# A fourth buffer for pairs of weight words, one pair loaded earlier in the first tile, and retention steps handed out more often in the second tile

## The chip, the core and the metric

The kernel runs on one core of a Trainium2 chip. The metric is device time in microseconds (us). A core has five engines that run at the same time and wait for each other through semaphores: TensorE (matmuls, PE in the profile, its weight loads PEld), VectorE (DVE), ScalarE (ACT), GpSimd (POOL) and SyncE (SP), which here only issues transfers. Each engine works through its own list of instructions strictly in the order in which the program wrote them; this program fixes that order by hand (a manual schedule). An instruction that has to wait holds up everything behind it on its engine.

## What is computed

The inputs are q, k and v of 8 batches, 8 heads, 576 positions and 64 dimensions, and four weight matrices. The first part is a retention layer (attention without a softmax, with a decay by distance), the second a feed-forward layer with a maximum over three projections:

```python
scores = (1 / np.sqrt(D)) * np.matmul(q, k.transpose(0, 1, 3, 2))
gamma = 1.0 - 2.0 ** (-5.0 - np.arange(H))
Dmat = np.where(rel >= 0, gamma[:, None, None] ** rel[None], 0.0)    # rel = position of q - position of k
attn = np.matmul(scores * Dmat[None], v)
x = attn.transpose(0, 2, 1, 3).reshape(B * S, H * D)                 # 4608 x 512
h = np.maximum(np.maximum(x @ w1, x @ w2), x @ w3)                   # w1..w3: 512 x 768
out = h @ w_out                                                      # w_out: 768 x 512
```

The weights arrive as 64-bit floats. The kernel reads them as pairs of 32-bit words ("bits") and converts them to 32-bit floats itself.

## The kernel before

**Tiles.** The 4608 rows of x are cut into nine tiles of 512 rows (`NT`), each made of four chunks of 128 rows (`CPT = 4`). While the feed-forward layer of tile t runs, the retention of tile t + 1 is computed between its matmuls. `steps(t + 1)` gives twelve slots with the retention's parts (`load`, `transposes`, `decay`, `scores`, `values`, ...), and the generator `ffn(t)` yields between them. The loop at the end of the program takes one slot, then lets `ffn` go on to its next yield. So the first tile's feed-forward (t = 0) runs with `steps(1)`, which has its own branch with chunks a, b, c, d = 4, 5, 6, 7 (lines 924 to 939). From chunk 7 on (`BY_PE`), q and k are transposed on VectorE out of blocks that `load_blocks` has fetched in small pieces (lines 214 and 221), one buffer pair each for q and k. Earlier chunks are transposed on TensorE.

**First tile: weights.** `pieces` lists the weights in blocks of 128 columns: 18 for the three projections, then 6 for w_out. Two blocks form a pair, 1 MB, which lies in one tile `bits` of the pool `wraw`; its buffers are `WAHEAD // 2`, which is 3. `load_weights(n)` (line 485) issues the next n blocks on SP, a projection block in two transfers (line 499), a block of w_out in one (line 494). Three pairs are loaded ahead of the first tile. After that, `product`, the last step of converting a pair, calls `load_weights`, so that each converted block starts the load of one block three pairs later. `convert_all` is the conversion as a generator: `exponent` (lines 630, 632), `fraction` (638, 639, 641), `whole` (644), `sign` (648) and `product` (656) for each pair, on VectorE and ScalarE; `ffn(0)` advances it between its matmul groups (`up_plain`, line 784) and then multiplies h by w_out (`downs_plain`, line 771). When all pairs are converted, the pools of the conversion are closed, and a pool called `late` takes over their memory, for sums of weights, of x and of h.

**Second tile and after: fewer products.** From tile 1 on, two of the three pairs of hidden blocks (in tile 1) or all three (later) are computed by `up`. It replaces a part of the block products by sums of blocks of x and of the weights: a list of 20 `PRODUCTS` in five accumulating chains named A to E (line 760). After a step of a chain, ScalarE copies the chain's bank to a tile `part` or into h (line 745), and VectorE joins such parts (line 748). Each product is two matmul pairs, and the generator `up` yields after each of them, so a hidden pair has 40 steps.

**Who hands out the retention's VectorE work.** From tile 1 on, `soon` does not issue a step of the retention at once but appends it to the queue `urgent` (`spread` is set). This holds for VectorE's transposes (line 194 by the profile, since they are issued from `chore`), the masks, the sums of states, the scaled values xT, the sums of x, and also for `load`, whose transfers then are issued by SP. `chore()` takes one step from `urgent`, or, when that is empty, from `chores` (sums of weights). In `ffn(t)` with t > 0, the loop over the steps of `up` decides when:

```python
elif step % 4 == 1 or step % 4 == 3 and len(urgent) > 6:
    chore(len(urgent) > 0)
elif step % 4 == 2 and chores and (t > 1 or NF // 2 - 1 not in summed_fp):
    chores.popleft()()
```

So one retention step is handed out at every fourth step, and a second one, two steps later, while more than six wait. Anything left over is handed out all at once ahead of the next `scores` or `values`. The order in which this happens is the order of VectorE's and SP's lists.

Of the kernel before, what the change touches and what calls it, by code (L numbers as in the profile page):

```python
# [77 lines left out]
WAHEAD = 6  # L78
# [3 lines left out]
def kernel(  # L82
# [32 lines left out]
    ppool = ctx.enter_context(tc.tile_pool(name="ppool", bufs=PARTS))  # L115
    opool = ctx.enter_context(tc.tile_pool(name="opool", bufs=2))
    while_converting = ExitStack()
    wraw = while_converting.enter_context(tc.tile_pool(name="wraw", bufs=WAHEAD // 2))
    wtmp = while_converting.enter_context(tc.tile_pool(name="wtmp", bufs=2))
    raw0 = while_converting.enter_context(tc.tile_pool(name="raw0", bufs=1))  # L120
    ps_r = ctx.enter_context(tc.tile_pool(name="ps_r", bufs=4, space=PSUM))
# [63 lines left out]
    late, chores, urgent, scaling, spread = {}, deque(), deque(), deque(), []  # L185

    def scale(n=1):
        for _ in range(min(n, len(scaling))):
            scaling.popleft()()  # L189

    def chore(n=1):
        for _ in range(n):
            if urgent or chores:
                (urgent or chores).popleft()()
# [59 lines left out]
    def transposes(g):  # L254
        both = qks[g] = {}
        if g >= BY_CHUNKS:
            for n, tag in (("k", "kT"), ("q", "m1")):
                both[n] = att.tile([P, H, D], FP32, tag=tag, name=n + "T", bufs=2 if n == "k" else 3)
        else:
            both["k"] = att.tile([P, NP, C], FP32, tag="kT", name="kT", bufs=2)  # L260
            both["q"] = ppool.tile([P, NP, C], FP32, tag="part", name="qT")
        if g >= BY_PE:
            for n in ("k", "q"):
                soon(partial(nc.vector.transpose, both[n][:].rearrange("a p c -> a (p c)"),
                             raws.pop(("kx" if n == "k" else n, g))[:].rearrange("a x y i -> a (x y i)")))
            return
        for n, src in (("k", raws["k", g]), ("q", raws.pop(("q", g)))):
            pool, tag = (ps_r, "r") if g >= CPT else (ps_x, "x")
            pt = pool.tile([P, NP, C], FP32, tag=tag, name=n + "t")
            for p in range(NP):  # L270
                nc.tensor.transpose(pt[:, p, :], pair(src, p), ident[:C, :C])
            nc.scalar.copy(both[n][:], pt[:])
# [449 lines left out]
    def late_room():  # L722
        pool = late["pool"]
        late["W"] = [pool.tile([P, NF, P], FP32, name=f"n{n}") for n in range(1, 9)]
        late["X"] = {n: pool.tile([P, NH], FP32, name=n)[:] for n in sorted({x[0] for x in X_SUMS})}
# [3 lines left out]
    def convert(n):  # L729
        for _ in range(n):  # L730
            next(converting, None)
# [47 lines left out]
    def up_plain(t, h, fb, i):  # L779
        ps = (ps_x, ps_y)[fb % 2].tile([P, NT], FP32, tag="xy"[fb % 2], name="up")  # L780
        first_of_all = t == 0 and (fb, i) == (0, 0)
        for cols in (slice(0, NT - C), slice(NT - C, NT)) if first_of_all else (slice(0, NT),):
            for dc in range(NDC):
                nc.tensor.matmul(ps[:, cols], lhsT=w_sb[i, fb][:, dc * P:(dc + 1) * P], rhs=xT[t][:, dc, cols],  # L784
                                 start=dc == 0 and cols.start == 0, stop=dc == NDC - 1,
                                 skip_group_check=first_of_all)
        if i > 0:
            return lambda: nc.vector.tensor_tensor(h[:, fb, :], h[:, fb, :], ps[:], op=ALU.max)
        return lambda: nc.scalar.copy(h[:, fb, :], ps[:])

    def ffn(t):

        h = hpool.tile([P, NF, NT], FP32, tag="h", name="h")
        if t == 0:
            for fp, i in units:
                for fb in (2 * fp, 2 * fp + 1):
                    maximum = up_plain(t, h, fb, i)
                    if CPT not in qks:
                        maximum()
                        transposes(CPT)  # L800
                        convert(4)
                        continue
                    if (fp, i) == units[-1]:
                        maximum()
                        convert(2)
                        continue
                    convert(4 if (fp, i) in units[:2] else 2)
                    maximum()
                yield
            convert(3)  # L810
            for fb, _ in enumerate(downs_plain(t, h)):
                convert(2 if fb < 2 else 4 * len(pieces))
                if fb == 2:
                    while_converting.close()
                    late["pool"] = ctx.enter_context(tc.tile_pool(name="late", bufs=1))
                    late_room()
                    sums_of_outs()
                elif fb > 2:
                    chore({3: 4, 4: 0, 5: 2}[fb])
                if fb in (1, 3):  # L820
                    yield
            yield
            return
        if t == 1:
            spread.append(True)
            weight_sums(0)
            weight_sums(2)
        plain = 1 if t == 1 else None
        order = (1, 0, 2) if t == 1 else (0, 2, 1)
        total = sum(48 if fp == plain else 2 * len(PRODUCTS) for fp in order)  # L830
        count = parts = 0
        for fp in order:
            if fp != plain:
                while fp not in summed_fp:
                    chore()
            for step, cost in enumerate(up_plain_all(t, h, fp) if fp == plain else up(t, h, fp)):
                if fp == plain:
                    chore(4 if step == 4 else 8)
                elif step % 4 == 1 or step % 4 == 3 and len(urgent) > 6:
                    chore(len(urgent) > 0)  # L840
                elif step % 4 == 2 and chores and (t > 1 or NF // 2 - 1 not in summed_fp):
                    chores.popleft()()
                if step % 3 == 2:
                    scale()
                count += cost or 1
                if count * (NF // 2 * 3) >= (parts + 1) * total:
                    parts += 1
                    yield
            sums_of_hidden(h, fp)
            if fp == plain:  # L850
                weight_sums(fp)
        chore(len(urgent))
        for n, _ in enumerate(downs(t, h, order)):
            chore(4)
            scale(2)
            if n in (1, 3):
                yield
        yield
# [52 lines left out]
    def steps(t):  # L911


        todo = [[] for _ in range(3 * CPT)]

        def at(n, *what):
            for step, *args in what:
                if step is values:
                    if args[0][0] < NG:
                        todo[n].append(partial(values, *args))  # L920
                elif args[0] < NG:
                    todo[n].append(partial(soon, partial(step, *args)) if step is load else partial(step, *args))

        if t == 1:
            a, b, c, d = range(CPT, 2 * CPT)
            at(0, (load, b))
            at(1, (scores, a), (state, a), (keep, a))
            at(2, (transposes, b), (decay, b), (load, c))
            at(3, (scores, b), (load_blocks, d, 0))
            at(4, (decay, c), (load_blocks, d, 1, 2))  # L930
            at(5, (values, [a, b], [b, c]), (load_blocks, d, 3), (load, d))
            at(6, (keep, c), (transposes, c), (load_blocks, d + 1, 0))
            at(7, (transposes, d), (decay, d), (load_blocks, d + 1, 1, 2))
            at(8, (scores, c), (scores, d), (load_blocks, d + 1, 3), (load, d + 1))
            at(9, (load_blocks, d + 2, 0, 1))
            at(10, (decay, d + 1), (load_blocks, d + 2, 2))
            at(11, (values, [c, d], [d]), (load_blocks, d + 2, 3), (load, d + 2),
               (transposes, d + 1))
            return todo
        for n in range(0, CPT, 2):  # L940
            a, b, m = CPT * t + n, CPT * t + n + 1, 6 * (n // 2)
            first_pair = a == BY_CHUNKS
            s = m + 2 if first_pair else m + 1
            at(m - (t == 2 and n > 0), (transposes, b))
            if first_pair:
                at(m, (decay, b), (load, a + 2), (carry, a))
            at(s, (scores, a), (scores, b), (load, b + 2))
            at(s + 1, (decay, a + 2))
            at(s + 2, (decay, b + 2))
            at(s + 3, (values, [a, b]), (transposes, a + 2), (load, a + 4))  # L950
        return todo
# [58 lines left out]
```

## Time and profile before

| what | value |
|---|---|
| median of 4 runs | 756.0 us (755.84 to 757.13) |
| the profiled execution's own time | 757.13 us |
| its span, first to last instruction | 755.1 us |
| granted TensorE clock | 1.000 |
| TensorE busy | 744.3 us (99% of the span) |
| VectorE busy | 509.1 us (67%) |
| ScalarE busy | 319.5 us (42%) |
| GpSimd busy | 82.2 us (11%) |
| first tile's feed-forward, first up matmul to last down matmul | about 27 to 126 us |
| second tile | about 126 to 209 us |
| transfers in the first 60 us | 217 to 225 GB/s, the 16 transfer engines 96 to 100% busy |

In a timeline line the columns are: start in us, duration in us, engine, line, operation, what is written and read, tile shapes, and how many instructions were merged; in square brackets, the idle time of the engine just before it and what ended that idle time. A line of the table of waits reads: who waited, for whom, us in total, how often, and the longest. "SPq" is the issuing of a transfer on SP.

### The profile page before, as it was taken

The numbers are of one execution on the slowest core, as the hardware profiler recorded it, in microseconds if no ns is written. First come the engines' busy times: TensorE is split into PE (matmuls) and PEld (weight loads), VectorE is DVE, ScalarE is ACT, GpSimd is POOL, SyncE is SP. The second block draws the span as 40 slices with busy tenths as digits, with TensorE's granted clock in tenths as the row PEclk, the third lists the DMA queues.
The fourth block names the chain that finished last, engine by engine and source line by source line (L and its number), as shares of the span: only waits on it lengthen the run. The fifth ranks groups of instructions, "written<-read, shape, count | busy, mean of one in ns | idle before, by whom it ended". The sixth has DMA issues, their size and how long they took to land.

```text
span 755.1 us, 16567 instructions
## 1 busy us (share of the span) xinstructions
PE 744.3 (99%) x6728; PEld 607.5 (80%) x6728; DVE 509.1 (67%) x856; ACT 319.5 (42%) x645; POOL 82.2 (11%) x103
## 2 busy tenths in 40 slices
PE   7999999999999999999999999999999999999998
PEld 6645545588888888888888888888888888888887
DVE  2898897858876866677567647675667656763662
ACT  3575531064245443544355435542454245414441
POOL 3110113001000110011010101010101010100000
PEclk9999999999999999999999999999999999999999
DMA  9995762504242414242243324142415141000001
GB/s 214 225 237 122 203 145 68 101 2 79 64 99 43 82 46 100 56 72 56 69 88 63 64 60 95 32 83 63 88 35 98 43 93 36 1 30 29 0 1 56
DMA packets 230204, 59.30 MB, mean 79 GB/s; under 512 B 210800, under 2 KB 228848, under 8 KB 230128
## 3 DMA queue, kind: packets, MB, share of 16 engines
q1 hardware_dynamic: 229264, 57.91, 35.4%
q8 instruction: 53, 0.87, 0.5%
q10 hardware_dynamic: 864, 0.33, 0.2%
q14 instruction: 23, 0.19, 0.1%
HBM read 48.76 MB, written 9.44 MB: 77 GB/s over the span
## 4 chain that ended last, share of the span: by engine, by line
PE 95%; DVE 2%; DMA 2%; SPq 1%; issue 0%; ACT 0%; ACTq 0%; DVEq 0%
PE a L760 18%; PE b L760 15%; PE dx L557 11%; PE up L784 11%; PE c L760 8%; PE dz L557 5%; PE d L760 5%; PE e L760 5%; PE sk L307 3%; PE down L771 3%; PE dy L557 3%; PE o L424 2%; PE o L431 2%; DMA qraw<-in_q_dram 1%; PE kv L310 1%; PE s L285 1%
## 5 line engine op out<-in xcount | busy, mean ns | idle before, releaser
L748 DVE TENSOR_TENSOR part<-part 128x512 f32<-128x512 f32 x161 | 111.2, 691 | 108.4 <-ACT part L745 106.0
L745 ACT COPY part<-b 128x512 f32<-128x512 f32 x115 | 67.3, 586 | 154.7 <-PE b L760 154.7
L748 DVE TENSOR_TENSOR h<-h,part 128x512 f32<-128x512 f32 x115 | 80.3, 698 | 29.3 <-ACT h L745 25.4
L784 PE MATMUL up<-xT,w 128*128 128x512 f32 (+2 forms) x200 | 84.8, 579 | 1.5 <-DVE w L656 1.5
L745 ACT COPY part<-a 128x512 f32<-128x512 f32 x92 | 53.9, 585 | 49.6 <-PE a L760 49.1
L784 PEld LDWEIGHTS up<-xT,w 128*128 128x128 f32 x200 | 36.7, 190 | 43.7 <-issue 39.9
L760 PE MATMUL a<-s,w 128*128 128x256 f32 x276 | 70.9, 380 | 0.0
L760 PE MATMUL b<-s,n 128*128 128x256 f32 x276 | 70.8, 379 | 0.0
L189 ACT ACTIVATE vraw<-vraw,gk 128x64 f32<-128x64 f32 x208 | 65.6, 346 | 3.5 <-DMA vraw<-in_v_dram 3.4
L760 PEld LDWEIGHTS b<-s,n 128*128 128x128 f32 x276 | 52.5, 190 | 7.1
L760 PEld LDWEIGHTS a<-s,w 128*128 128x128 f32 x276 | 52.4, 190 | 7.1
L527 POOL TENSOR_TENSOR H<-h 128x256 f32<-128x256 f32 x24 | 20.2, 842 | 308.7 <-DVE h L748 308.7
L760 PE MATMUL c<-xT,w 128*128 128x256 f32 x184 | 49.1, 389 | 0.0
L760 PE MATMUL b<-xT,n 128*128 128x256 f32 x184 | 47.2, 379 | 0.0
L760 PE MATMUL d<-s,w 128*128 128x256 f32 x184 | 47.2, 379 | 0.0
L324 POOL TENSOR_TENSOR s<-s,gs_of 64x512 f32<-64x512 f32 x21 | 22.2, 1055 | 213.7 <-DVE s L322 209.2
L557 PE MATMUL dx<-To,H 128*128 128x256 f32 (+1 forms) x204 | 44.9, 371 | 0.0
L760 PE MATMUL e<-xT,w 128*128 128x256 f32 x184 | 43.5, 379 | 0.0
L760 PE MATMUL a<-xT,n 128*128 128x256 f32 x184 | 43.5, 379 | 0.0
L557 PEld LDWEIGHTS dx<-To,H 128*128 128x128 f32 x204 | 36.6, 190 | 4.8
L760 PEld LDWEIGHTS e<-xT,w 128*128 128x128 f32 x184 | 35.0, 190 | 5.2 <-DVE s L322 0.2
L760 PEld LDWEIGHTS b<-xT,n 128*128 128x128 f32 x184 | 35.0, 190 | 4.7
(122 smaller groups left out, 1283.8 us busy)
## 6 DMA issues: line engine op xcount, KB each, us to landing
bits<-in_moe_w_dram SPq DMA_DIRECT2D x36, 256.0 KB, 5.4
out_dram<-osb SPq DMA_DIRECT2D x35, 256.0 KB, 2.1
kraw<-in_k_dram SPq DMA_DIRECT2D x32, 256.0 KB, 3.2
vraw<-in_v_dram SPq DMA_DIRECT2D x32, 256.0 KB, 3.6
qraw<-in_q_dram SPq DMA_DIRECT2D x224, 32.0 KB, 2.2
kxraw<-in_k_dram SPq DMA_DIRECT2D x224, 32.0 KB, 2.1
bits<-in_moe_w_out_dram SPq DMA_DIRECT2D x6, 512.0 KB, 5.9
qraw<-in_q_dram SPq DMA_DIRECT2D x6, 256.0 KB, 5.3
```

The lines of the kernel that those rows point to most:

```text
L189: scaling.popleft()()
L307: nc.tensor.matmul(s[half(c), h, :], lhsT=kT[half(c), h, :], rhs=qT[half(c), h, :], start=True, stop=True)
L324: nc.gpsimd.tensor_tensor(new, new, factor, op=ALU.mult)
L424: nc.tensor.matmul(o[m][half(c), n, u, :], lhsT=vds[g][half(m), h, :], rhs=sts[g][half(m), h, :], start=n == 0 and u == 0, stop=place(g, m ...
L431: nc.tensor.matmul(o[m][half(c), n, u, :], lhsT=stacks[g][half(m), h, :], rhs=qks[g]["q"][half(m), h, :], start=False, stop=True, skip_gro ...
L527: urgent.append(lambda: (pool(s3, a11, a21, op=ALU.subtract), pool(s4, a12, s2, op=ALU.subtract)))
L557: nc.tensor.matmul(o, lhsT=hS[n](fp)[:, m * P:(m + 1) * P], rhs=late["T"][n][:, fp, cols], start=first and fp == order[0] and (m == 0 or l ...
L745: nc.scalar.copy(of[step], ps[step[0]][:])
L748: nc.vector.tensor_tensor(of[dst], a, b, op=op)
L760: nc.tensor.matmul(ps[chain][:, e, :], lhsT=factor(w, 2 * fp + e), rhs=xS[t][x], start=n == 1 and e == 0, stop=ends, skip_group_check=True)
L771: nc.tensor.matmul(b[:], lhsT=h[:, fb, m * P:(m + 1) * P], rhs=w_sb["out", fb], start=(fb == 0), stop=(fb == NF - 1))
L784: nc.tensor.matmul(ps[:, cols], lhsT=w_sb[i, fb][:, dc * P:(dc + 1) * P], rhs=xT[t][:, dc, cols], start=dc == 0 and cols.start == 0, stop= ...
```

## The change

Three edits:

- The pool `wraw` has four buffers for pairs of weight words instead of three (`WAHEAD // 2 + 1`).
- In the third slot of `steps(1)`, during the first tile's feed-forward, `load_weights(2)` loads one more pair right after chunk c's load. From there on, each load of a pair is for the pair four ahead of the one just converted, instead of three ahead.
- In the second tile (t = 1) alone, the second retention step of every four is handed out while more than two wait, not only while more than six wait. In the other tiles the bound stays six.

```diff
-    wraw = while_converting.enter_context(tc.tile_pool(name="wraw", bufs=WAHEAD // 2))
+    wraw = while_converting.enter_context(tc.tile_pool(name="wraw", bufs=WAHEAD // 2 + 1))
...
-                elif step % 4 == 1 or step % 4 == 3 and len(urgent) > 6:
+                elif step % 4 == 1 or step % 4 == 3 and len(urgent) > (2 if t == 1 else 6):
                     chore(len(urgent) > 0)
...
-            at(2, (transposes, b), (decay, b), (load, c))
+            at(2, (transposes, b), (decay, b), (load, c), (load_weights, 2))
```

No arithmetic changes, and no instruction is added or taken away on TensorE, VectorE, ScalarE or GpSimd.

## The prediction

> **What bounds the kernel now.** I read the page first (busy shares, then the chain that ended last), then TensorE's own waits in the second tile and after, then the timelines of TensorE, VectorE and the SP queue around each of those waits.
>
> From the page, engine shares and the chain by engine:
>
> ```profile
> PE 744.3 (99%) x6728; PEld 607.5 (80%) x6728; DVE 509.1 (67%) x856; ACT 319.5 (42%) x645; POOL 82.2 (11%) x103
> ...
> PE 95%; DVE 2%; DMA 2%; SPq 1%; issue 0%; ACT 0%; ACTq 0%; DVEq 0%
> ```
>
> TensorE is the bound: 95% of the last chain is its work. A busy PE row says little by itself, because matmul ends are modelled, but the chain runs from one matmul group straight into the next nearly everywhere. So a change that removes no matmul can only win the places where TensorE waits. TensorE's waits from 125 us to the end are a single line:
>
> ```profile
> PE sk L307 <- DVE qT L194: 1.0, 1, 1.0
> ```
>
> One wait in 630 us. In the timeline of TensorE it stands between the two chunks whose scores are computed in the middle of the second tile:
>
> ```profile
> 174.12 0.23 PE L310 MATMUL kv<-vraw,kraw 64*64 64x64 f32 x2
> 175.39 0.33 PE L307 MATMUL sk<-qT,kT 64*64 64x64 f32 x3 [1.04 <-DVE qT L194]
> ```
>
> The page counts 1.04 us idle, from the modelled end of one matmul. These small matmuls follow each other about every 0.06 us (the pair before starts at 174.11), so without the wait the second chunk would start at 174.17. The slot lost is 175.39 - 174.17 = 1.22 us. TensorE's weight loads wait 1.2 us for the same qT.
>
> VectorE's timeline ahead of it shows why qT is late:
>
> ```profile
> 163.29 1.28 DVE L194 TENSOR_TENSOR xT<-o,gq 128x512 f32<-128x512 f32 x2
> 166.14 2.14 DVE L748 TENSOR_TENSOR part<-part 128x512 f32<-128x512 f32 x3 [1.56 <-ACT part L745]
> 168.20 0.70 DVE L194 STREAM_TRANSPOSE kT<-kxraw 128x512 f32<-128x512 f32 x1
> 168.82 0.65 DVE L748 TENSOR_TENSOR h<-h,part 128x512 f32<-128x512 f32 x1
> 169.40 1.41 DVE L748 TENSOR_TENSOR part<-part 128x512 f32<-128x512 f32 x2
> 170.72 0.70 DVE L194 STREAM_TRANSPOSE qT<-qraw 128x512 f32<-128x512 f32 x1
> 171.35 2.17 DVE L748 TENSOR_TENSOR h<-h,part 128x512 f32<-128x512 f32 x3
> 173.44 0.68 DVE L748 TENSOR_TENSOR part<-e,part 128x512 f32<-128x512 f32 x1
> 174.04 0.70 DVE L194 STREAM_TRANSPOSE kT<-kxraw 128x512 f32<-128x512 f32 x1
> 174.66 0.67 DVE L194 STREAM_TRANSPOSE qT<-qraw 128x512 f32<-128x512 f32 x1
> ```
>
> VectorE works in order and is full from 166.14 to 175.26. Just before, it is idle 1.56 us for an ACT copy. The four transposes are the retention steps that line 839 hands out.
>
> **Second edit, the retention steps.** It adds no instruction. In the built order of the changed kernel the first chunk's kT and qT stand right behind the two xT, ahead of the three part sums; the second kT stands ahead of the three h joins, the second qT behind them. Working through with the starts above (start to start: transpose 0.62, one h 0.60, two parts 1.32, three h 2.09):
> - First pair: 164.5 to 165.8, wholly inside the 1.56 us of idle, so the part sums still start at 166.14. Their inputs were issued on SP by 146 us and land in 2 to 3 us, so the early place waits for no transfer.
> - Then three parts to 168.20, h to 168.80, two parts to 170.12, second kT to 170.74, three h to 172.83, second qT to 173.46.
> - 173.46 is 0.71 us before TensorE can use it (174.17). The wait goes: 1.22 us.
>
> A rule speaks against it. The third h join also releases a GpSimd difference (H L527, 0.73 us), which in the new order runs beside that second qT. The Trainium skill, "SBUF — State Buffer", section "Who interferes with whom", says VectorE and GpSimd share a port pair as an exclusive lock, the loser blocked for a whole instruction, for VectorE's two-port modes and its two-input operations. The trace shows such a case: an h join at 178.36 takes 1.51 us instead of 0.69 beside a GpSimd multiply at 178.28. Were qT held so, it would end at 173.46 + 0.73 = 174.19 and the gain be 1.2 less 0.02 plus a semaphore's 0.05, about 1.15. But transposes at 124.88 to 127.49 run beside GpSimd work and keep 0.70 and 0.67, so I take the row: 1.22. What may be held is the H sum behind it, 0.3 us, and that is covered.
>
> What becomes late: the e join moves from 173.44 to about 173.9. Its bank is wanted by chain d at 182.72 (181.5 after the gain), over 6 us of cover; with that cover gone it would cost its 0.5. SP's next loads wait for the first qT and are issued near 166 instead of 171.45; their data, and the values that ACT scales, come earlier, and ACT has idle time for them. From 187.00 VectorE's run starts from an ACT copy of TensorE's own output, so it shifts along with TensorE and no new wait appears.
>
> **First edit, the fourth buffer and the early load.** It adds 8 KB a partition and no transfer; every pair from the eighth on is issued one place earlier. What is late now is this (VectorE's timeline, then SP's; the DMA wait is for the first output weights):
>
> ```profile
> 88.02 0.69 DVE L630 TENSOR_SCALAR expo<-bits 128x1024 int32<-128x1024 int32 x1 [2.31 <-DMA bits<-in_moe_w_out_dram]
> ...
> 97.56 0.69 DVE L788 TENSOR_TENSOR h<-h,up 128x512 f32<-128x512 f32 x1 [0.93 <-PE up L784]
> 98.16 0.69 DVE L630 TENSOR_SCALAR expo<-bits 128x1024 int32<-128x1024 int32 x1
> 98.77 1.23 DVE L648 SCALAR_TENSOR_TENSOR expo<-bits,expo 128x1024 int32<-128x1024 int32 x1
> 100.03 1.23 DVE L656 TENSOR_TENSOR w_out<-mant,expo 128x1024 f32<-128x1024 f32 x1
> ```
> ```profile
> 60.08 2.97 SPq L499 DMA_DIRECT2D bits<-in_moe_w_dram  x4
> 63.10 4.36 SPq L214 DMA_DIRECT2D qraw<-in_q_dram  x8
> ```
>
> - Gained off the path: VectorE's waits for bits, 0.70 (at 79.46) and 2.31 us, and ACT's of 0.60, 2.37 and 1.41, should vanish. None is on TensorE's path. VectorE then only waits longer at the next point that TensorE sets: the max at 97.56.
> - The one TensorE wait near, 0.35 us at 101.31 for the first w_out, stays: it is max end of up (97.54) to product (101.26), 3.72 us in a row on VectorE, and the change moves none of these instructions. The bound from above, if it did go, is the start-to-start loss: 93.82 + 6.97 (a group of 16) = 100.79 against 101.31, 0.5 us.
> - The first loads into the fourth buffer (near 30 us) no longer wait for VectorE; SP's waits on line 499 are 3.0 us in all (2.1 and 0.9). The transfer engines are full until 60 us, so the order of arrival is as before: nothing.
> - Cost on SP: four more issues, 2.97 us, ahead of chunk 7's blocks (54.88 on). The blocks end two issues late: 79.6 + 1.2 = 80.8, and land at 83.0 by the median of 2.2. VectorE wants them at 84.42 (83.7 once the 0.70 is gone), TensorE the transposes at 91.84, 6.1 us after they end now (85.72). Covered. Their bytes are 1 MB; at the mean of 207 GB/s from 45 to 65 us that is 5.1 us of transfer. "DMA: Bandwidth & Descriptors", section "Measured", gives 6.15 us for 1 MB: an estimate by it adds one more microsecond, and both leave the path untouched.
>
> **Sum.** 1.22 + 0 = 1.2 us, between 0 (the gap refills elsewhere) and 1.7 (both gaps). The profiled execution took 757.13 us around a span of 755.1; its span becomes 753.9, its time 755.9. It is the slowest of four; against the median of 756.0 I forecast 754.8, or -0.16%. About 0.2% (1.5 us) is what a measurement of this kernel can tell from no change.
>
> **Rivals.**
> - The gap refills, or was particular to this execution (the other three are 1.0 to 1.3 us faster than it): gain 0 to 0.6, 755.4 to 756.0. For it: VectorE carries the same work, only in another order. Against: 0.71 us of margin, and no other TensorE wait for 500 us.
> - More than counted: the 0.5 at 101.31 goes too, or the second chunk's matmuls (1.19 us against 0.99 for the first) run as the first: 1.7, so 754.3. Against: the 3.72 us of VectorE do not move.
> - Slower: the early bits delay chunk 7's blocks. It decides once they land after 90.5 (then kT and qT end past 91.84), 7.5 us behind the 83.0 expected; to end 1.5 us above now it must also eat the 1.2, landing near 93.2: 757.6 or more. For it: the longest such block took 7.1 us to land. Against: even that lands at 87.9.
>
> **How the numbers follow.** Forecast case 0.70, by itself 754.4 to 755.2; refill 0.15; more 0.08; slower 0.07. The range of 754.2 to 756.3 leaves the slow case and little else out. Faster by over 0.2% needs below 754.5: the "more" case and the lower edge of the forecast, 0.21. Slower than 757.5: 0.07. The rest, 0.72, within.
>
> **What would show it.** Right: no wait of sk for qT near 174; transposes at 164.5 to 165.8, part sums still near 166.1; no VectorE wait for bits of the output weights; the 0.35 at the first down still there; SP's loads of the third tile from near 166. Wrong: a new TensorE wait before 126 us, part sums pushed past 166.5, or a wait for a bank after 176.

## The result, and the profile after

| | before | after |
|---|---|---|
| median, us | 756.3 (755.11 to 759.18) | 755.0 (753.70 to 757.81) |
| ratio of the times, with its 95% interval | | 0.9983 [0.9977, 0.9988] |
| span of the profiled execution, us | 755.1 | 752.7 |
| its own time, us | 757.13 | 754.70 |

The kernel became faster by 0.17%, 1.3 us. The forecast was 754.8 us, or 0.16% less.

The two profiled executions differ by more than that, 2.4 us of span, so the first step is to see where the difference lies. I cut TensorE's timeline at its landmarks. "First up" is the first product of the feed-forward layer, "first down" the first product with w_out, "sk" and "a" are where the second tile computes both chunks' scores and goes on to the next chain, and "last dx" is the start of the last run of products with w_out, whose bank is called dx:

| from, to | before | after | difference |
|---|---|---|---|
| start of the span to first up | 26.87 | 25.50 | -1.37 |
| first up to first down | 74.44 | 74.44 | 0.00 |
| first down to the second tile's first up | 24.29 | 24.30 | +0.01 |
| to the first sk | 47.58 | 47.58 | 0.00 |
| first sk to the next chain a (the scores of two chunks) | 3.40 | 2.02 | -1.38 |
| to the last dx | 572.92 | 572.90 | -0.02 |
| the tail behind it | 5.60 | 5.96 | +0.36 |

I don't count the start as the change's doing. Until the first up both kernels issue the same work. In the execution of before, TensorE waited 1.93 us for the third chunk's q to arrive; in that of after it didn't. This start lay at 25.6 to 26.9 us in the five profiles with three buffers and at 24.7 to 26.1 in the nine with four, so the profiles alone would leave room for an effect of the buffer. The times speak against it: the buffer alone gains nothing (below). I take as the profile's own answer the sum of the five middle rows, -1.39 us, 0.18% of 756, which is the measured ratio. All of it lies in one row.

The page of after, engine shares and the chain by engine, says as little about this as before's did:

```profile
PE 745.0 (99%) x6728; PEld 608.8 (81%) x6728; DVE 509.6 (68%) x856; ACT 319.1 (42%) x645; POOL 83.5 (11%) x103
...
PE 96%; DVE 1%; DMA 1%; issue 1%; SPq 0%; ACT 0%; ACTq 0%; DVEq 0%
```

TensorE's table of waits for the whole span of after (who waited, for whom, us in total, times, longest) does:

```profile
PE up L784 <- DVE w L656: 1.5, 1, 1.5
PE warm L153 <- POOL ident masks.py:199: 1.4, 1, 1.4
PE s L285 <- ACT qT L272: 0.6, 1, 0.6
PE o L393 <- POOL vd L249: 0.5, 1, 0.5
PE down L771 <- DVE w_out L656: 0.4, 1, 0.4
PE o L393 <- PE kv L352: 0.2, 1, 0.2
```

The row of sk waiting for qT is gone and no row of the second tile has taken its place: the two waits of o, which before's table does not have, lie ahead of the first up. The row of the first down is still there. VectorE's timeline around the second tile's transposes:

```profile
161.93 1.28 DVE L194 TENSOR_TENSOR xT<-o,gq 128x512 f32<-128x512 f32 x2
163.13 0.70 DVE L194 STREAM_TRANSPOSE kT<-kxraw 128x512 f32<-128x512 f32 x1
163.75 0.67 DVE L194 STREAM_TRANSPOSE qT<-qraw 128x512 f32<-128x512 f32 x1
164.77 2.14 DVE L748 TENSOR_TENSOR part<-part 128x512 f32<-128x512 f32 x3 [0.35 <-ACT part L745]
166.95 0.69 DVE L748 TENSOR_TENSOR h<-h,part 128x512 f32<-128x512 f32 x1
167.56 1.41 DVE L748 TENSOR_TENSOR part<-part 128x512 f32<-128x512 f32 x2
168.89 0.70 DVE L194 STREAM_TRANSPOSE kT<-kxraw 128x512 f32<-128x512 f32 x1
169.52 2.17 DVE L748 TENSOR_TENSOR h<-h,part 128x512 f32<-128x512 f32 x3
171.61 0.70 DVE L194 STREAM_TRANSPOSE qT<-qraw 128x512 f32<-128x512 f32 x1
172.24 0.55 DVE L525 TENSOR_TENSOR H<-h 128x256 f32<-128x256 f32 x1
172.71 0.68 DVE L748 TENSOR_TENSOR part<-e,part 128x512 f32<-128x512 f32 x1
```

Take 1.37 us off every predicted time, for the earlier start. Then the first pair was due at 163.1 to 164.4 and ran from 163.13 to 164.42. The part sums were due at 164.77 and started there: the transposes used up idle time, of which 0.35 us is left of 1.56. The second qT was due to end at 172.09 and ended at 172.31.

TensorE's timeline, at the first down and at the second chunk's scores:

```profile
99.94 14.00 PE L771 MATMUL down<-w_out,h 128*128 128x512 f32 x32 [0.37 <-DVE w_out L656]
...
172.74 0.23 PE L307 MATMUL sk<-qT,kT 64*64 64x64 f32 x2
172.80 0.22 PE L307 MATMUL sk<-qT,kT 64*64 64x64 f32 x2
```

The sk follow each other at 0.06 us. TensorE reaches them at 172.74, so qT has 0.43 us to spare.

In the first tile, VectorE's timeline of after:

```profile
83.88 0.66 DVE L630 TENSOR_SCALAR expo<-bits 128x1024 int32<-128x1024 int32 x1
...
96.17 0.69 DVE L788 TENSOR_TENSOR h<-h,up 128x512 f32<-128x512 f32 x1 [2.05 <-PE up L784]
96.78 0.69 DVE L630 TENSOR_SCALAR expo<-bits 128x1024 int32<-128x1024 int32 x1
97.38 1.25 DVE L648 SCALAR_TENSOR_TENSOR expo<-bits,expo 128x1024 int32<-128x1024 int32 x1
98.66 1.23 DVE L656 TENSOR_TENSOR w_out<-mant,expo 128x1024 f32<-128x1024 f32 x1
```

The exponent at 83.88 is the one that waited 2.31 us for bits before. It waits for nothing now, and the time comes back as idle time at the next point that TensorE sets: 2.05 us ahead of the max, where it was 0.93. The row from max to product is as long as it was, and the first down still waits 0.37 us for it.

### The profile page after: what moved, and what is told of

It is laid out like the page before. It is cut to its first block, busy times and chain, and to the rows that moved or that the text cites. A ratio compares the mean times of both kernels' runs of the same rounds, so it can differ in the third digit from the quotient of the medians.

```text
span 752.7 us, 16566 instructions
## 1 busy us (share of the span) xinstructions
PE 745.0 (99%) x6728; PEld 608.8 (81%) x6728; DVE 509.6 (68%) x856; ACT 319.1 (42%) x645; POOL 83.5 (11%) x103
## 4 chain that ended last, share of the span: by engine, by line
PE 96%; DVE 1%; DMA 1%; issue 1%; SPq 0%; ACT 0%; ACTq 0%; DVEq 0%
PE a L760 19%; PE b L760 16%; PE up L784 11%; PE dx L557 11%; PE c L760 8%; PE e L760 5%; PE d L760 5%; PE dz L557 5%; PE sk L307 3%; PE down L771 3%; PE dy L557 3%; PE o L424 2%; PE o L431 2%; PE s L285 1%; PE kv L310 1%; PE o L393 1%
## 5 line engine op out<-in xcount | busy, mean ns | idle before, releaser
L760 PEld LDWEIGHTS a<-xT,n 128*128 128x128 f32 x184 | 35.0, 190 | 4.7
```

What stands on the lines that cost most here:

```text
L760: nc.tensor.matmul(ps[chain][:, e, :], lhsT=factor(w, 2 * fp + e), rhs=xS[t][x], start=n == 1 and e == 0, stop=ends, skip_group_check=True)
```

## The experiments

No kernel here leaves out any of the computation. Ratios are times of the named kernel over the kernel before, with their 95% intervals.

### Each edit by itself

As in the prediction, "the first edit" is the fourth buffer together with the early load, and "the second edit" is the retention steps. (The two expectations below count the three changes one by one.)

The retention steps alone (three buffers, no early load):

```diff
-elif step % 4 == 1 or step % 4 == 3 and len(urgent) > 6:
+elif step % 4 == 1 or step % 4 == 3 and len(urgent) > (2 if t == 1 else 6):
```

> Only the third edit: the second retention step of every four is handed out while more than two wait, in the second tile; three buffers, no early load. If the whole gain is the wait of sk for qT (my theory): TensorE's wait near 174 us gone, ratio to before about 0.9983 (755.0 us against 756.3), the same as the whole change. If the fourth buffer carries the gain: ratio 1.000. If the two share it: about 0.9992.

The buffer and the early load alone:

```diff
-wraw = ...tc.tile_pool(name="wraw", bufs=WAHEAD // 2)
+wraw = ...tc.tile_pool(name="wraw", bufs=WAHEAD // 2 + 1)
-at(2, (transposes, b), (decay, b), (load, c))
+at(2, (transposes, b), (decay, b), (load, c), (load_weights, 2))
```

> Only the first two edits: four buffers and the early load. My theory: ratio 1.000 within 0.0005; VectorE's 2.31 us wait for the output weights gone, the 1.04 us wait of sk for qT still there, the 0.35 us at the first down still there. If the early load carries part of the gain: ratio 0.9990 or lower.

Measured: the steps alone 755.49 us, 0.9985 [0.9978, 0.9991]; the buffer alone 756.60 us, 1.0009 [0.9997, 1.0021]. The buffer's ratio is pulled up by two of its fourteen executions, at 760.1 and 760.8 us; its median is that of before beside it (756.55). The scores of the two chunks took 2.03 us with the steps alone and 3.38 with the buffer alone (before 3.40). So the gain of the second tile is the second edit's, and the first edit by itself gains nothing. Nor was the wait particular to one execution: in the profile of every kernel here that keeps the bound of six these scores took about 3.4 us. Both edits together, measured again beside the last group of kernels below, gave 755.09 us, 0.9979 [0.9971, 0.9987].

> The changed kernel itself on the same chip as the other three: ratio to before 0.9983 as on record.

The timelines of VectorE and of TensorE for the steps alone show what the first edit might yet be good for:

```profile
88.98 0.69 DVE L630 TENSOR_SCALAR expo<-bits 128x1024 int32<-128x1024 int32 x1 [2.83 <-DMA bits<-in_moe_w_out_dram]
...
97.50 0.67 DVE L788 TENSOR_TENSOR h<-h,up 128x512 f32<-128x512 f32 x1
...
101.23 1.98 PE L771 MATMUL down<-w_out,h 128*128 128x512 f32 x4 [0.73 <-DVE w_out L656]
```

With three buffers VectorE waited 2.83 us for the bits here (2.31 in before's execution). Counted from the first up, they came 1.4 us later than in before's (88.98 - 26.40 for 88.02 - 26.87). The max has no idle time ahead of it: the lateness has used up VectorE's slack of 0.93, and the first down waits 0.73 instead of 0.35. So "none is on TensorE's path" held by under 1 us in before's execution, and no longer in this one. The fourth buffer is a cover for such executions. How often they occur, one profile for each kernel can't say, and between 0.9985 and 0.9983 the times don't tell either.

### Half of the second edit

If the gain is the lateness of one transpose, a bound between six and two must give a part of it that the order of VectorE's list foretells. With four, the second qT stands behind the e join, but its kT is early:

```diff
-elif step % 4 == 1 or step % 4 == 3 and len(urgent) > 6:
+elif step % 4 == 1 or step % 4 == 3 and len(urgent) > (4 if t == 1 else 6):
```

> The kernel before with the bound at four instead of six in the second tile: the first kT comes ahead of the part sums, but the second qT comes behind the e join. A middle dose. By the same adding-up as in the prediction: three parts at 166.14, qT to 168.82, h, two parts, three h to 172.83, kT to 173.45, e join to 174.05, qT to 174.65, against 174.17 wanted. So TensorE should still wait about 0.5 us at sk (start to start), and about 0.7 us be gained: ratio 0.9991. If the gain came from anything but the end of that qT, it would be 0 or the whole 1.2.

Measured: 756.0 us, 0.9990 [0.9984, 0.9997]. From the timelines of VectorE and of TensorE:

```profile
172.32 0.65 DVE L748 TENSOR_TENSOR part<-e,part 128x512 f32<-128x512 f32 x1
172.90 0.69 DVE L194 STREAM_TRANSPOSE qT<-qraw 128x512 f32<-128x512 f32 x1
...
173.64 0.32 PE L307 MATMUL sk<-qT,kT 64*64 64x64 f32 x3 [0.45 <-DVE qT L194]
```

The wait is 0.45 us, and the scores of both chunks take 2.80 us: a gain of 0.60, where after gains 1.38. The rival that the gap refills in another place falls with this: half the lateness gave about half of the gain in the trace. The time agrees, but its interval is too wide to tell a half from nearly the whole.

### The rival that ends slower: chunk 7's blocks late

To delay the blocks without changing the work of the other engines, extra transfers of 128 KB stand on SP right behind the early pair. Everything behind them on SP is late too, weights included. They fill a tile that nobody reads, one after the other, since all write the same place (with four of them, SP waits 8.5 us in three places for the one before to land):

```diff
+junk = const.tile([P, DM // 2], FP32, name="junk")
+def load_junk(n):
+    for _ in range(n):
+        nc.sync.dma_start(junk[:].rearrange("p (h d) -> p h d", d=D),
+                          q[0, 0:4, 0:P, :].rearrange("h p d -> p h d"))
...
-at(2, (transposes, b), (decay, b), (load, c), (load_weights, 2))
+at(2, (transposes, b), (decay, b), (load, c), (load_weights, 2), (load_junk, n))
```

With n = 2, 4 and 8 (these kernels' line numbers are 6 higher from there on):

> The changed kernel with two extra transfers of 128 KB ahead of chunk 7's blocks, about 5 us by what four and eight cost on SP (10.4 and 20.3 us). The blocks then land near 87 to 88, ahead of 90.5, where the slower rival decides: TensorE waits for neither scores nor weights, and the time is that of the changed kernel, ratio about 0.9985. If the room were smaller than counted: above 1.000, with a TensorE wait between 77 and 97 us.

> The changed kernel with four extra transfers of 128 KB on SP, one after the other into one scratch tile that nobody reads, right behind the early pair and ahead of chunk 7's blocks. It measures how much room the early load has (the slower rival). Each takes about 3 us from issue to landing, so SP is held about 10 us. The rival's sum: blocks then land near 93 instead of 83, 2.5 us past its point of decision at 90.5, and TensorE's scores wait about 2 to 3 us: ratio to before about 1.001 to 1.003. If the queue has more idle time than I counted: as the changed kernel, 0.998.

> The same with eight extra transfers, about 20 us. The rival's sum: blocks land near 103, and TensorE waits about 12 us for chunk 7's scores, or loses as much for late weights: ratio to before about 1.014. If the delay is soaked up: under 1.005.

And four of them in the kernel before, with three buffers and no early pair (`(load, c), (load_junk, 4)`):

> The kernel before with the same four extra transfers at the same place (behind chunk c's load): three buffers, no early pair. It asks what the fourth buffer buys when transfers are late. If it is only room: here the weights' words come 10 us late as well, VectorE waits for them as it already did (2.3 us), and the loss is larger than with four buffers: 5 to 8 us over before, ratio 1.007 to 1.010. If the fourth buffer is of no use even then: the same loss as e3_junk4 against its own kernel, 3 to 4 us.

| | ratio to before | chunk 7's kT starts | first up to first down |
|---|---|---|---|
| after | 0.9983 [0.9977, 0.9988] | 82.66 | 74.44 |
| after, 2 transfers | 0.9979 [0.9969, 0.9988] | 85.50, after 3.23 of waiting | 74.94 |
| after, 4 transfers | 1.0059 [1.0045, 1.0073] | 91.57, after 7.09 of waiting | 80.88 |
| after, 8 transfers | 1.0176 [1.0162, 1.0190] | 100.79, after 7.05 of waiting | 89.19 |
| before, 4 transfers | 1.0104 [1.0089, 1.0120] | 92.46 | 83.23 |

Two transfers cost nothing that the times can tell. (The first down came 0.50 us later in that profile; two profiles of the changed kernel itself differ there by 0.88.) Four bring the blocks past the point where, by the prediction, the rival decides (90.5), and it does decide: the kernel is slower than before. So the point lies between the two, and its exact place is taken up in the part on the prediction. The price was wrong: I had expected 1.001 to 1.003. The timelines of VectorE and of TensorE with four transfers:

```profile
91.57 0.71 DVE L201 STREAM_TRANSPOSE kT<-kxraw 128x512 f32<-128x512 f32 x1 [7.09 <-DMA kxraw<-in_k_dram]
...
90.56 1.16 PE L285 MATMUL s<-qT,kT 64*128 64x128 f32 x16
92.93 1.16 PE L285 MATMUL s<-qT,kT 64*128 64x128 f32 x16 [1.20 <-DVE qT L201]
95.99 9.91 PE L790 MATMUL up<-xT,w 128*128 128x512 f32 x16 [1.90 <-DVE w L662]
```

TensorE pays three times. It waits 1.20 us for the transposes. It waits 1.90 for w, because the conversion of the next pair stands behind the transposes in VectorE's list: 7.09 us of waiting in one place made all of VectorE's later work late. And then 16 matmuls take 9.91 us, which take 7.13 when TensorE runs at full speed. The table of stretches of the same execution (stretch in us, its length, busy us and count of PE, PEld, DVE, ACT and POOL, then the granted TensorE clock, the DMA share and GB/s) has the reason:

```profile
92.00:96.00 4.00, 1.17 (x17) 1.01 (x17) 3.97 (x6) 2.30 (x2) 0.69 (x1) 0.85 1.07 288
96.00:99.00 3.00, 3.00 (x4) 1.45 (x5) 2.90 (x4) 0.94 (x1) 0.74 (x1) 0.50 1.11 344
99.00:102.00 3.00, 3.00 (x5) 1.16 (x5) 2.62 (x5) 0.29 (x1) 0.00 (x0) 0.56 0.93 249
102.00:106.00 4.00, 3.90 (x10) 1.40 (x8) 3.46 (x4) 2.14 (x2) 0.00 (x0) 1.00 0.47 87
```

In the first stretch TensorE is busy for 1.17 of 4 us. Its mean clock of 0.85 is 1.2 us at half, so the clock fell at 94.8 us, inside the second of the two pauses, and by the mean of 0.56 it stayed at half until 101.6. The up matmuls ran 5.6 us of this time, without a pause. The Trainium skill, "TensorE: Matmul & The Clock Gate", Part 1, tells of such a gate: half rate after an idle window of about 3.4 us, full rate after a busy one, the windows running freely. The length agrees, since 6.8 us is two such windows. The condition is looser here: in the 3.4 us before the fall TensorE had not been idle, but busy for 1.5 us. The price of the three together is 1.20 + 1.90 + 2.78 = 5.9 us. The measured one is (1.0059 - 0.9983) x 756 = 5.7. (By the table, this one execution lost 6.4 us up to the first down: the idle times undercount the two stalls, as they did at sk.)

With eight transfers it is late weights that stop TensorE, before it ever gets to chunk 7's scores, which wait for nothing. TensorE's timeline:

```profile
84.54 16.73 PE L790 MATMUL up<-xT,w 128*128 128x512 f32 x32 [7.32 <-DVE w L662]
105.94 8.80 PE L790 MATMUL up<-xT,w 128*128 128x512 f32 x16 [2.62 <-DVE w L662]
```

Every pair behind the extra transfers on SP is late. Besides the 9.94 us of waiting, the slow clock adds 16.73 - 13.90 = 2.83 and 8.80 - 7.13 = 1.67. The sum is 14.4 us, and (1.0176 - 0.9983) x 756 = 14.6. I had again left out the clock, which here fell even after a single pause of 2.62 us.

The kernel before, with the same four transfers, lost 7.9 us (1.0104), while the changed one lost 5.7. In it TensorE waits 5.4 us for w in three places of the first tile, the longest here, and the slow clock behind it adds 9.82 - 7.13 = 2.7:

```profile
90.67 9.82 PE L790 MATMUL up<-xT,w 128*128 128x512 f32 x16 [4.18 <-DVE w L662]
```

So the first edit does what it says when transfers are late: it saves about 2 us, give or take 1.6 by the intervals. SP was held for less in the kernel before, 8.58 us by four transfers against 10.41. In the unchanged flow of transfers there is no such lateness for it to cover.

### The wait that both edits leave: the first down

The prediction put the 0.35 us at the first down to a row on VectorE: max, exponent, sign, product. The max isn't needed by the product. Behind the last pair of up, I let the conversion go first:

```diff
                     if (fp, i) == units[-1]:
-                        maximum()
                         convert(2)
+                        maximum()
                         continue
```

In the changed kernel:

> The changed kernel, with one more edit: in the last unit of the first tile the conversion of the first output weights is issued ahead of the max, not behind it. It tests why the 0.35 us wait of the first down stayed. My theory: it is VectorE's chain of max, exponent, sign, product (3.72 us) behind the end of the first half of the last up; without the max in front the chain can start about 2 us earlier, the wait goes and 0.4 to 0.5 us more is gained: ratio to before about 0.9977, span near 0.5 us below the changed kernel's from the first up on. Rival: the transfer of the output weights sets it, and nothing is gained over the change.

In the kernel before:

> The kernel before with only the order of the last unit swapped: conversion of the first output weights ahead of the max, three buffers, no early load, bound six. It asks whether the wait of the first down needs the fourth buffer to go. If VectorE's order alone sets it: the 0.35 to 0.7 us wait at the first down goes here too, ratio to before about 0.9994. If the late bits (2.3 to 2.8 us of VectorE wait at three buffers) hold the chain when the max no longer does: the wait stays and the ratio is 1.000.

In the kernel before with the fourth buffer and the early pair, without the second edit:

> The kernel before with the fourth buffer, the early pair, and the conversion of the first output weights ahead of the max in the last unit; bound six. It tells whether the fourth buffer is worth anything once VectorE's order lets it: with three buffers that order gained nothing (1.0004 to 0.9987 times before), because the late words moved the wait of 0.3 us from the first output weights to h. If with four buffers the wait goes for good: 0.4 to 0.5 us gained, ratio about 0.9994. If the order gains nothing in any case: 1.000.

And once more in the changed kernel:

> The changed kernel with the conversion ahead of the max, measured again beside the changed kernel itself. If the gains add: 0.4 to 0.5 us under the changed kernel, ratio to before about 0.9977. If the first measurement (0.9969) was right in full: 1 us under it.

| swap in | time, us | ratio to before | without the swap |
|---|---|---|---|
| before | 756.41 | 0.9996 [0.9987, 1.0005] | 1 |
| before with the first edit | 755.06 | 0.9983 [0.9977, 0.9990] | 1.0009 [0.9997, 1.0021] |
| after | 754.23 | 0.9969 [0.9957, 0.9981] | 0.9983 [0.9977, 0.9988] |
| after, again | 753.71 | 0.9964 [0.9951, 0.9976] | 0.9979 [0.9971, 0.9987] |

In both measurements the changed kernel with the swap is faster than before, and lower than without it; against the latter the intervals, with only five executions of the swap each time, overlap a little. Its timelines of VectorE and of TensorE:

```profile
94.55 0.68 DVE L630 TENSOR_SCALAR expo<-bits 128x1024 int32<-128x1024 int32 x1
...
96.40 1.23 DVE L656 TENSOR_TENSOR w_out<-mant,expo 128x1024 f32<-128x1024 f32 x1
97.54 0.68 DVE L788 TENSOR_TENSOR h<-h,up 128x512 f32<-128x512 f32 x1
...
99.91 3.60 PE L771 MATMUL down<-w_out,h 128*128 128x512 f32 x8
```

The product is done 2.3 us before it is wanted, in time that VectorE had been idle, and the first down waits for nothing. In the kernel before the same swap gains nothing that can be measured, and its timelines of VectorE, GpSimd and TensorE show what became of it:

```profile
87.69 0.69 DVE L630 TENSOR_SCALAR expo<-bits 128x1024 int32<-128x1024 int32 x1 [2.10 <-DMA bits<-in_moe_w_out_dram]
...
99.83 1.57 POOL L249 TENSOR_TENSOR vraw<-vraw,gk 128x512 f32<-128x512 f32 x1 [14.55 <-DMA vraw<-in_v_dram]
...
100.60 1.88 DVE L644 SCALAR_TENSOR_TENSOR mant<-frac,mant 128x1024 f32<-128x1024 int32 x1
102.41 0.67 DVE L788 TENSOR_TENSOR h<-h,up 128x512 f32<-128x512 f32 x1
...
103.13 11.43 PE L771 MATMUL down<-w_out,h 128*128 128x512 f32 x26 [0.31 <-DVE h L788]
```

The first down starts in time, and three microseconds later TensorE waits 0.31 us for another max: the wait has moved. Two things lie behind it. With three buffers VectorE has lost 2.10 us to late bits ahead of this place, and has no idle time left. And the step of the conversion just ahead of that max takes 1.88 us, where the same step took 1.23 in the changed kernel with the swap; GpSimd's decay of v runs beside it. The 0.65 lost there is more than the wait. With four buffers and the swap, in the kernel without the second edit, the same step also took 1.88 beside the decay, and TensorE waited for nothing, since VectorE was earlier. So, as far as these runs go, the swap needs the buffer: the first edit gives 0 (1.0009), the swap 0 (0.9996), both together a gain (0.9983). The interval of the swap alone still allows a gain of 1 us.

The swap's gain with four buffers, 0.14 to 0.15% or 1.1 us in the changed kernel, is too large for a wait of 0.37 us; the first profiles of the two kernels differ by 0.5 us from first up to last dx. A part of the difference lies in the repeated profile of the changed kernel. Its timelines of GpSimd, VectorE and TensorE at the first down:

```profile
98.28 1.04 POOL L249 TENSOR_TENSOR vraw<-vraw,gk 128x512 f32<-128x512 f32 x1 [12.06 <-DMA vraw<-in_v_dram]
...
98.30 2.11 DVE L656 TENSOR_TENSOR w_out<-mant,expo 128x1024 f32<-128x1024 f32 x1
...
100.46 14.00 PE L771 MATMUL down<-w_out,h 128*128 128x512 f32 x32 [1.23 <-DVE w_out L656]
```

GpSimd's decay of v starts 0.02 us ahead of the product, and the product takes 2.11 us instead of 1.23. TensorE waits 1.23 us instead of 0.37. In the first profile of after, the decay started at 99.63, behind the product's start (98.66), and the product kept its 1.23. The Trainium skill, "SBUF — State Buffer", "Who interferes with whom", has the rule: a VectorE instruction with two inputs and a GpSimd instruction that reads exclude each other, and the one issued first holds the ports for its whole length. The row agrees nearly: 0.88 us lost, of the 1.02 that the decay had left. The opposite order agrees too: in the kernel before with four extra transfers the decay started 0.22 us behind the product, the product kept its 1.23, and the decay took 1.91. The decay starts when a transfer of v lands, between 97.7 and 102.0 us in the executions without extra transfers, so what it collides with changes from one to the next. With the swap in the changed kernel the product was over by 97.6, ahead of the earliest of them. What is shown is that one such collision cost TensorE 0.86 us at the first down. How often it happens, and so that it makes up the rest of the swap's gain, is argued. Whether the first edit makes it likelier is open: without the swap, the decay began 73.1 to 74.3 us behind the first up in three profiles with four buffers and 74.6 to 75.6 in three with three. The row of the first edit with the swap stays partly open: its own profile accounts for 0.66 us from first up to last dx, its median for 1.3.

## Why the prediction was right

**The second edit: right, by its own steps.** The wait of 1.22 us went, the four transposes stand where the order put them, and they fill the 1.56 us of idle. The edit alone gives 0.9985, 1.1 us. Half of the lateness gives about half of the gain.

**The margin was smaller than counted.** qT was to be 0.71 us early and was 0.43 us early. It came 0.22 us later than the sum of the starts (172.31 for 172.09), and TensorE came slightly sooner. Of the 0.22, 0.07 is a slip in the sum: it ended the last transpose 0.63 us after its start, where the result is there only after its whole 0.70.

**The row against the rule.** I had set a row (transposes keep 0.70 beside GpSimd) against the rule of the exclusive lock. GpSimd's difference did run beside the second qT, from 171.77, and qT kept its 0.70. The row decided rightly. And there was little conflict to weigh: the rule speaks of instructions with two inputs, and of the two-port modes, and a transpose has one input. Where the rule did bite was at the product of w_out, where I hadn't applied it.

**The size: 1.38 and not 1.22.** The remainder, 0.16, is the second rival's small term: the second chunk's matmuls took 1.19 us behind the stall and about 1.0 without it. It had been seen, and put down as a rival instead of a part of the wait's price. The other term of that rival, the first down, did not come.

**The number: closer than the sum deserves.** The medians differ by 1.3 us, and 1.2 was forecast. But the repeated profile of the changed kernel lost 0.88 us in the first tile (75.32 from first up to first down, for 74.44) to a collision that the prediction does not have, and single executions of the changed kernel spread over 4 us. That the medians came within 0.1 us of the forecast is luck in part; the row of the second tile is what confirms the sum.

**The first edit: right that it gains nothing, too sure of why.** VectorE's waits for bits went and came back ahead of the max (0.93 to 2.05), and the first down kept its wait. Two details fell. ScalarE's third wait was to vanish, and ScalarE still waits 1.82 us at 89.48 for the second pair of w_out; VectorE takes that pair up only later, so it costs nothing. And "none is on TensorE's path" was read from a single execution, in which the margin was 0.93 us. In the execution with three buffers and the second edit alone, it was used up. The blocks of chunk 7 were also issued later than summed: SP was done with them at 80.54, 2.3 us later than before (79.60) once the start's 1.37 is taken off, where the sum had 1.2. It was covered. The 6.15 us that "DMA: Bandwidth & Descriptors", section "Measured", gives for 1 MB is for a transfer issued by GpSimd, while SP issues these in four pieces, which landed 4.6 to 7.0 us after their issue; the figure decided nothing.

**The slower rival: the point a microsecond early, the price wrong.** At a landing of 85.5 nothing, at 91.57 a loss. But 90.5 was worked out from the start of the 32 score matmuls at 91.84, and the first 16 of these are chunk 6's: with four transfers they run at 90.56 without a wait, and only the second 16 wait. TensorE wants chunk 7's transposes 1.0 us later, so the point is near 91.5. With the two first ups set equal, kT came at 93.1 in before's time, 1.6 us past this point, and TensorE lost 1.37 us from start to start. The price was worked out as the microseconds that the transposes come late, 1.20 with four transfers. What stands behind them on VectorE, and the clock, made it 5.7. The rival itself did not come true: with the early pair chunk 7's kT started at 82.66, earlier than before (84.42) by 0.4 us more than the start explains, since VectorE no longer stood waiting for bits ahead of it.

## What to carry to other kernels

Where one engine is the bound and another works in order, look for an idle time shortly ahead of the work that is late, and move the late work into it: here a bound in a scheduler's queue was worth about 1.1 us without one instruction less. A deeper buffer that only removes waits off the path gains nothing by itself, but it can be the condition for a reordering that needs the slack, so try both together before dropping either. Before a change of a tenth of a per cent is explained, cut the span at landmarks: 1.4 of the 2.4 us between these two profiles lay in the start, where one transfer came late.

## What was not expected of the hardware

- The clock fell to 0.50 within the second of two idle times, 1.20 and 1.90 us, with 1.16 us of small matmuls between them, none of them as long as the window of 3.4 us; elsewhere a single pause of 2.62 us was enough. The stall of 1.04 us in the second tile alone does not do this. Waits that cost 3.1 us by themselves then cost 5.9.
- A VectorE product issued 0.02 us behind a GpSimd multiply lost 0.88 us, and one issued 0.97 us ahead of it lost nothing.
- Small transfers into the same place held SP for 2.1 to 2.6 us each: four took 10.41 us of SP's timeline in the changed kernel and 8.58 in the kernel before, eight took 20.29.
